# Strassen's seven products for the second MLP product of an attention and MLP kernel, with smaller input rings and a new order

## The chip, the core and the metric

The kernel runs on one core of one Trainium2 chip. The core has a matrix engine (PE), a vector engine (DVE), a scalar engine (ACT), a general engine (POOL) and a queue engine (SP) that here issues transfers. Each engine works through its own instructions in order and waits for the others by semaphores. PE reads SBUF and writes PSUM, which has eight banks; the other engines empty PSUM. The metric is the time of one execution on the device in microseconds (us), as the median of several runs.

## The reference

What is computed, cut to what matters:

```python
# q, k, v: [8, 12, 448, 64]; w_in: [768, 2048]; w_out: [2048, 768]
q_n, k_n = rmsnorm(q, g_q), rmsnorm(k, g_k)
attn = softmax(q_n @ k_n.T / 8)
x = (attn @ v).transpose(0, 2, 1, 3).reshape(3584, 768)
h = x @ w_in
g = h * np.clip(h + 3.0, 0.0, 6.0) / 6.0
return (g @ w_out).astype(np.float32)          # [3584, 768]
```

Eight sequences of 448 tokens with twelve heads of 64 go through attention, and the 3,584 tokens through an MLP of 768 to 2,048 to 768. The "second product" is `g @ w_out`.

## The kernel before

The kernel describes itself as a list of small operations, each with the engines that could run it, what it reads and what it writes (`Plan.add`). Two long tables of numbers then decide everything: `ORDER` is the sequence in which the operations are emitted, and so the order of each engine's queue, and `WAY` picks the second or third of the possible engines where the first isn't used. Waits follow from what is read and written.

Work goes by pairs of heads: six pairs a sequence, 48 in all. For a pair, `load` (L425) brings q, k and v into rings of slots on SP's queue. `prep` squares q and k (L366 on POOL, L364 on ACT), sums the squares on DVE (L454), takes the inverse root on ACT (L430, L433) and scales to bf16 (`qks`, L369, on POOL or DVE). `trans` brings q and k into the layout `T` that PE needs: by PE and copies at first, by transfers from pair 13 on (L561). `score` multiplies (L594; two matmuls of 64 rows side by side), ACT takes the exponential (`eT`, L600), `av` multiplies with v (`X`, L680: 65 columns, the last one the softmax's sum), and `finish` divides on DVE (L696, L699) and transposes into `xT` (L706). The first sequence is treated in halves by functions ending in `_first`, with PE warmed by matmuls on zeros (L382). One line often serves many operations, since helpers such as `copy` (L350 on ACT, L352 on DVE) record them.

The MLP of sequence b runs while the attention of b+1 goes on. `h_group` (L772; L753 for the first sequence) makes 128 of the 2,048 hidden columns with six matmuls of 448 columns into a PSUM bank `M`; ACT applies `relu` (L731, into `ts`), DVE gates (L734) into `gT`, the activations in bf16, with the hidden dimension on partitions. `gT` is a ring of two buffers, each with two sequences: 896 tokens, seven tiles of 128. `y_group` (L794) makes one token tile's row of 768 outputs as two halves of 384 columns, each with 16 matmuls into one bank, in four pieces that `ORDER` can place apart. Each half is copied to a row buffer `y` (three of them), and the row is stored by several transfers (L815). Two banks serve hidden and output products alike, five in the last sequence. `mix` spreads a group's tiles evenly among the next sequence's hidden groups. The last tile's second half is done in two quarters of 192 columns.

Some buffers of the start live inside buffers used later: the first sequence's `T` and v, and two extra q/k slots, in the second `gT`, two extra v slots in `xT`.

Of the kernel before, what the change touches and what calls it, by code (L numbers as in the profile page):

```python
# [12 lines left out]
A_MIN = mybir.AluOpType.min  # L13
LN = mybir.ActivationFunctionType.Ln
# [191 lines left out]
def kernel(  # L206
# [11 lines left out]
    nc = tc.nc  # L218
# [53 lines left out]

    flat = gT_r[1][:].rearrange("p f s -> p (f s)")
    T0 = flat[:, 0:NPAIR * TW].rearrange("p (u c) -> p u c", c=TW)
    o0 = NPAIR * TW
    va0 = flat[0:TP, o0:o0 + NPAIR * 2 * T * E1].rearrange("p (u a t e) -> p u a t e", a=2, t=T, e=E1)
# [683 lines left out]
```

## Time and profile before

| | us |
|---|---|
| median of 3 runs (423.02 to 424.02) | 423.32 |
| profiled execution, first to last instruction | 421.4 |
| PE busy | 413.0 |
| ACT busy | 288.3 |
| PE weight loads busy | 243.8 |
| DVE busy | 233.1 |
| POOL busy | 168.8 |

The profile is one execution of its own. An engine's busy time is the union of its instructions' times; those of PE are pipelined, with modelled ends, so that its busy share alone doesn't tell how full it is. The chain of waits is followed back from the last instruction, at each step to what released it. A group's row names line, engine, operation, output and inputs, shape and count, then busy time, mean length of one in ns, and the idle time before them with what ended it.

### The profile page before, as it was taken

The page shows a single profiled execution, that of the slowest core. Times are in us where ns is not written, and L with a number is a line of the kernel's source. Part 1 is how long each engine was busy: PE and PEld are TensorE (multiplying, and loading weights), DVE is VectorE, ACT ScalarE, POOL GpSimd, SP SyncE. Part 2 cuts the span into 40 slices and gives each one's busy share as a digit, 9 for nine tenths or more (in the row PEclk, how much of TensorE's full clock was granted, in tenths as well). Part 3 has the DMA queues.
Part 4 walks back from the last instruction along what each step waited for, and adds up shares of the span by engine and source line. Part 5 has one row for each costly group of instructions (what it writes and reads, how often), then busy time and mean ns, then how long its engine had stood idle before and what let it go on. Part 6 is the DMA issues. An engine that isn't in the chain of part 4 may idle for free.

```text
span 421.4 us, 9981 instructions
## 1 busy us (share of the span) xinstructions
PE 413.0 (98%) x3959; PEld 243.8 (58%) x3960; DVE 233.1 (55%) x474; ACT 288.3 (68%) x527; POOL 168.8 (40%) x189
## 2 busy tenths in 40 slices
PE   7899999999999999999999999999999999999996
PEld 3566886555545555555555555555655556555565
DVE  5987776588875667536554754447345333333210
ACT  6999887678887988788767876677765662133201
POOL 3999596478374554427344143043210100000000
PEclk9999999999999999999999999999999999999999
DMA  7999999999779799568495683747350601120034
GB/s 241 319 282 196 258 216 177 275 268 271 178 194 252 193 252 242 111 154 211 115 224 160 164 206 73 135 154 166 82 93 12 143 2 47 30 81 27 8 107 114
DMA packets 98979, 67.77 MB, mean 161 GB/s; under 512 B 53204, under 2 KB 95476, under 8 KB 98932
## 3 DMA queue, kind: packets, MB, share of 16 engines
q1 hardware_dynamic: 93296, 60.50, 56.9%
q0 software_dynamic: 5248, 6.29, 9.0%
q8 instruction: 31, 0.51, 0.5%
q10 hardware_dynamic: 388, 0.34, 0.3%
q14 instruction: 16, 0.13, 0.1%
HBM read 50.23 MB, written 11.01 MB: 145 GB/s over the span
## 4 chain that ended last, share of the span: by engine, by line
PE 82%; DMA 7%; ACT 5%; DVE 2%; issue 1%; POOL 1%; SPq 1%; POOLq 0%; ACTq 0%; DVEq 0%
PE M L772 27%; PE M L794 25%; PE X L680 9%; PE S L594 5%; PE M L753 4%; DMA qk<-in_k_dram 4%; PE S L794 4%; PE X L594 3%; DMA T<-qks 2%; PE X L772 1%; ACT sq L364 1%; DMA out_dram<-y 1%; ACT eT L600 1%; ACT eT L622 1%; PE S L617 1%
## 5 line engine op out<-in xcount | busy, mean ns | idle before, releaser
L794 PE MATMUL M<-w_out_sb,gT 128*128 128x384 bf16 x752 | 139.3, 326 | 0.2 <-DMA w_out_sb<-in_moe_w_out_dram 0.2
L772 PE MATMUL M<-xT,w_in_sb 128*128 128x448 bf16 x618 | 135.0, 353 | 0.1
L369 POOL TENSOR_TENSOR qks<-qk,rs 112x512 bf16<-112x512 f32 (+1 forms) x91 | 91.0, 1019 | 107.3 <-ACT rs L433 77.2
L794 PEld LDWEIGHTS <-gT 128*128 128x128 bf16 x912 | 84.5, 98 | 59.5 <-issue 7.6
L734 DVE SCALAR_TENSOR_TENSOR gT<-ts,M 128x448 bf16<-128x448 f32 x119 | 73.2, 616 | 72.1 <-ACT ts L731 71.6
L600 ACT ACTIVATE eT<-S 112x896 bf16<-112x896 f32 x112 | 100.3, 915 | 15.7 <-PE S L594 8.5
L731 ACT ACTIVATE ts<-M 128x448 f32<-128x448 f32 x119 | 64.7, 545 | 42.7 <-PE M L772 29.2
L772 PEld LDWEIGHTS <-w_in_sb 128*128 128x128 bf16 x672 | 60.2, 98 | 56.3 <-issue 10.5
L366 POOL TENSOR_TENSOR sq<-qk 112x512 f32<-112x512 f32 (+1 forms) x57 | 58.0, 1024 | 52.9 <-DMA qk<-in_q_dram 29.7
L680 PEld LDWEIGHTS <-eT 112*128 112x128 bf16 x1344 | 52.7, 97 | 14.5 <-issue 2.0
L600 ACT ACTIVATE eT<-X 112x896 bf16<-112x896 f32 x56 | 51.3, 917 | 13.3 <-PE X L594 12.2
L680 PE MATMUL X<-va,eT 112*128 112x65 bf16 x1344 | 56.0, 194 | 0.1
L454 DVE TENSOR_REDUCE ssq<-sq 112x16 f32<-112x1024 f32 x42 | 50.9, 1213 | 6.1 <-POOL sq L366 4.7
L594 PE MATMUL S<-T 64*128 64x448 bf16 x224 | 34.0, 353 | 0.1
L352 DVE COPY y<-M 128x384 f32<-128x384 f32 x26 | 14.5, 556 | 30.9 <-PE M L794 30.8
L699 DVE TENSOR_TENSOR xn<-X,rd 112x512 bf16<-112x512 f32 x42 | 28.9, 689 | 1.3 <-DVE rd L696 0.2
L696 DVE RECIPROCAL rd<-X 112x8 f32<-112x8 f32 x42 | 8.6, 206 | 34.5 <-PE X L680 28.6
L594 PEld LDWEIGHTS <-T 64*128 64x128 bf16 x336 | 12.9, 94 | 24.5 <-issue 17.2
L364 ACT ACTIVATE sq<-qk 112x512 f32<-112x512 f32 (+1 forms) x40 | 23.0, 586 | 2.8 <-DMA qk<-in_k_dram 2.5
L350 ACT COPY y<-M 128x384 f32<-128x384 f32 x21 | 10.0, 477 | 19.4 <-PE M L794 19.2
L753 PE MATMUL M<-xT,w_in_sb 128*128 128x224 bf16 x192 | 22.9, 259 | 0.0
L794 PE MATMUL S<-w_out_sb,gT 128*128 128x384 bf16 (+1 forms) x128 | 22.6, 316 | 0.0
(87 smaller groups left out, 300.9 us busy)
## 6 DMA issues: line engine op xcount, KB each, us to landing
qk<-in_k_dram SPq DMA_DIRECT2D x45, 256.0 KB, 4.8
qk<-in_q_dram SPq DMA_DIRECT2D x45, 256.0 KB, 4.7
vf<-in_v_dram SPq DMA_DIRECT2D x43, 256.0 KB, 4.8
w_in_sb<-in_moe_w_in_dram POOLq DMA_DIRECT2D x4, 768.0 KB, 8.4
w_out_sb<-in_moe_w_out_dram POOLq DMA_DIRECT2D x4, 768.0 KB, 9.5
out_dram<-y SPq DMA_DIRECT2D x7, 336.0 KB, 3.5
out_dram<-y SPq DMA_DIRECT2D x8, 288.0 KB, 3.3
out_dram<-y SPq DMA_DIRECT2D x8, 240.0 KB, 2.8
```

What stands on the lines that cost most here:

```text
L366: em(nc.gpsimd.tensor_tensor(out=out, in0=in_, in1=in_, op=A_MULT))
L369: em((nc.vector if e == DVE else nc.gpsimd).tensor_tensor(out=out, in0=in_, in1=by.unsqueeze(3).to_broadcast(list(in_.shape)), op=A_MULT))
L454: em(nc.vector.tensor_reduce(out=ssq[:].rearrange("p i n -> p (i n)"), in_=sq[:].rearrange("p i (n d) -> p (i n) d", d=D), axis=AX_X, op=A ...
L594: em(nc.tensor.matmul(out=ps[:, a, 0:S], lhsT=qkT[r, S + t * TP:S + t * TP + 128], rhs=qkT[r, 0:S], start=True, stop=True))
L600: em(nc.scalar.activation(out=eT[:, t, 0:S2].rearrange("p (a s) -> p a s", a=2), in_=ps[0:TP, :, 0:S], func=EXP, bias=0.0, scale=1.0))
L680: em(nc.tensor.matmul(out=X_ps[:, a, i * E1:(i + 1) * E1], lhsT=eT[:, t, c:c + 128], rhs=va[:, a, t, :], start=(t == 0 and i == 0), stop=( ...
L699: em(nc.vector.tensor_tensor(out=xn[:].rearrange("p i a d -> p a i d"), in0=view()[:, :, :, 0:D], in1=rd[:].unsqueeze(3).to_broadcast([TP, ...
L731: em(nc.scalar.activation(out=ts[:], in_=ps()[:, 0:S], func=RELU, bias=0.5, scale=1.0 / 6.0))
L734: em(nc.vector.scalar_tensor_tensor(out=out, in0=shape(ts[:]), scalar=1.0, in1=shape(ps()[:, 0:S]), op0=A_MIN, op1=A_MULT))
L753: em(nc.tensor.matmul(out=ps()[:, f * SH:(f + 1) * SH], lhsT=w_in_sb[:, kt, f0:f0 + 128], rhs=xT[:, kt, z * SH:(z + 1) * SH], start=(kt == ...
L772: em(nc.tensor.matmul(out=ps()[:, 0:S], lhsT=w_in_sb[:, kt, f * 128:(f + 1) * 128], rhs=xT[:, kt, :], start=(kt == 0), stop=(kt == NKT - 1)))
L794: em(nc.tensor.matmul(out=ps()[:, 0:nc0], lhsT=gT[:, f, i * 128:(i + 1) * 128], rhs=w_out_sb[:, f, c0:c0 + nc0], start=(f == 0), stop=(f = ...
```

## The change

For a pair of token tiles, the second product is a 2 x 2 block product: the rows are the tiles i1 and i2, the inner blocks the two halves of the hidden dimension, the columns the two halves of the output. Strassen's scheme makes it with seven products of 8 matmuls of 384 columns each, instead of eight, and needs sums of the operands. A group's seven tiles make three pairs and a single one; the single uses the same changed weights with four products.

- `wsums`: ten sums and differences of blocks of `w_out`, once, of 4 x 384 elements a partition: three new buffers `wb`, and two blocks of `w_out` overwritten in place (`B12`, `B21`).
- `gsum`: five sums of activations for a pair and one for a single, 8 x 128 elements a partition, in bf16, on DVE or POOL; two go to a ring of two buffers `ga`, three in place into `gT`.
- Four products of a pair accumulate two by two in one bank that is read in between; of the outputs some are copied out of PSUM, some added to a row buffer by DVE, and two are differences of row buffers, on POOL or DVE.
- `gT` becomes one buffer with three sequences, in which odd sequences always take the middle third; the start's guests move to the last two thirds. To make room, the q/k ring goes from 5 + 1 slots and 2 extra to 4 + 1 and 1, the v ring from 5 + 1 and 2 to 3 + 1 and 2, and later loads are planned one pair nearer to their use for v.
- `zero_t` is half as wide and read twice. Squares name their two halves as a dimension of their own.
- `mix` takes pairs in portions of 4, 1, 1 and 1 products. `ORDER` and `WAY` are new throughout, for attention and loads also.

The core of the diff (the two tables, the moved guests and renamings left out):

```diff
-    NQK, NV, NSQ, NRS, NQS, NVA, NT, NE, NXN, NXT, NTS, NY = 5, 5, 2, 4, 3, 4, 4, 2, 2, 2, 2, 3
-    NQX = 2
+    NQK, NV, NSQ, NRS, NQS, NVA, NT, NE, NXN, NXT, NTS, NY = 4, 3, 2, 4, 3, 4, 4, 2, 2, 2, 2, 3
+    NG, NC, HF = 3, 2, NFT // 2
+    NQX, NVX = 1, 2
...
-    def y_group(g, i, nb):
...
-        for n, (c0, nc0) in enumerate(cols):
-            ps, res = bank(nb)
-            for part in range(4):
-                def f_y(_, part=part, ps=ps, c0=c0, nc0=nc0):
-                    for f in range(part * 4, part * 4 + 4):
-                        em(nc.tensor.matmul(
-                            out=ps()[:, 0:nc0], lhsT=gT[:, f, i * 128:(i + 1) * 128],
-                            rhs=w_out_sb[:, f, c0:c0 + nc0],
-                            start=(f == 0), stop=(f == NFT - 1)))
...
+    def wsums():
+        fs = HF // 2
+        for j in range(2):
...
+            for n, (o, x, y, op, reads, writes) in enumerate((
+                    (wb[:, 1, lo], b11, b12, A_ADD, [rl], [("wb", 1, j)]),
+                    (wb[:, 2, lo], b21, b22, A_ADD, [rh], [("wb", 2, j)]),
+                    (b12, b12, b22, A_SUB, [rl, rh, ("wb", 1, j)], [("w12", j)]),
+                    (b21, b21, b11, A_SUB, [rl, rh, ("wb", 2, j)], [("w21", j)]),
+                    (wb[:, 0, lo], b11, b22, A_ADD, [rl, rh], [("wb", 0, j)]))):
+                def f_w(e, o=o, x=x, y=y, op=op):
+                    em((nc.vector if e == DVE else nc.gpsimd).tensor_tensor(out=o, in0=x, in1=y, op=op))
+                plan.add("wb", [DVE, POOL], f_w, reads, writes)
...
+    def gsum(g, o, x, y, op, res):
+        def rows(i, k):
+            return gT[:, k * HF:(k + 1) * HF, g_tile(g, i):g_tile(g, i) + 128]
+        out = ga_r[o][:] if isinstance(o, int) else rows(*o)
...
+        def f_s(e):
+            em((nc.vector if e == DVE else nc.gpsimd).tensor_tensor(out=out, in0=rows(*x), in1=rows(*y), op=op))
+        plan.add("ga", [DVE, POOL], f_s, [r for t in (x, y) for f in raw(g, *t)[1] for r in f], wr)
...
+    def product(bk, ab, start=True, stop=True, c0=0, nc0=HALF):
+        ps, res = bk
+        (lhs, rl), (rhs, rr) = ab
+        for j in range(2):
+            def f_y(_, j=j):
+                for f in range(j * 4, j * 4 + 4):
+                    em(nc.tensor.matmul(
+                        out=ps()[:, 0:nc0], lhsT=lhs[f], rhs=rhs[f][:, c0:c0 + nc0],
+                        start=(start and f == 0), stop=(f == HF - 1), skip_group_check=True))
+            plan.add(f"y{nc0}", [PE], f_y, [r for f in range(j * 4, j * 4 + 4) for r in rl[f]] + rr(j), [res])
...
+    def y_add(dst, bk):
+        def f_a(_):
+            em(nc.vector.tensor_tensor(out=dst[0], in0=bk[0]()[:, 0:HALF], in1=dst[0], op=A_ADD))
+        plan.add("yt", [DVE], f_a, [bk[1], dst[1]], [dst[1]])
+    def y_sub(dst, x, y):
+        def f_a(e):
+            em((nc.vector if e == DVE else nc.gpsimd).tensor_tensor(out=dst[0], in0=x[0], in1=y[0], op=A_SUB))
+        plan.add("yu", [POOL, DVE], f_a, [x[1], y[1]], [dst[1]])
...
+    def y_pair(g, i1, i2, nb):
+        row1, row2 = y_row(False), y_row(True)
+        c11, c12, c21, c22 = half(row1, 0), half(row1, 1), half(row2, 0), half(row2, 1)
+        k = [bank(nb), bank(nb)]
+        a6 = gsum(g, 0, (i2, 0), (i1, 0), A_SUB, None)
+        a7 = gsum(g, 1, (i1, 1), (i2, 1), A_SUB, None)
+        a11, a22 = raw(g, i1, 0), raw(g, i2, 1)
+        product(k[0], (a11, B12))
+        y_copy(c22, k[0])
+        product(k[1], (a22, B21))
+        y_add(c22, k[1])
+        a5 = gsum(g, (i1, 1), (i1, 0), (i1, 1), A_ADD, None)
+        a2 = gsum(g, (i2, 0), (i2, 0), (i2, 1), A_ADD, None)
+        product(k[0], (a5, B22), start=False)
+        y_copy(c12, k[0])
+        product(k[1], (a2, B11), start=False)
+        y_copy(c21, k[1])
+        aS = gsum(g, (i1, 0), (i1, 0), (i2, 1), A_ADD, None)
+        yield 4
+        k = bank(nb)
+        product(k, (aS, BSUM))
+        y_add(c22, k)
+        y_sub(c11, c22, c12)
+        y_sub(c22, c22, c21)
+        yield 1
+        k = bank(nb)
+        product(k, (a7, B7))
+        y_add(c11, k)
+        y_store(g, i1, row1, (0, DM))
+        yield 1
+        k = bank(nb)
+        product(k, (a6, B6))
+        y_add(c22, k)
+        y_store(g, i2, row2, (0, DM))
+        yield 1
+    def y_single(g, i, nb, final):
+        row = y_row(True)
+        aS = gsum(g, 0, (i, 0), (i, 1), A_ADD, None)
+        a1, a2 = raw(g, i, 0), raw(g, i, 1)
+        for n, cols in enumerate([[(0, HALF)], [(0, HALF // 2), (HALF // 2, HALF // 2)] if final else [(0, HALF)]]):
+            for c0, nc0 in cols:
+                k = bank(nb)
+                product(k, (a1, B12) if n else (a2, B21), c0=c0, nc0=nc0)
+                product(k, (aS, B22 if n else B11), start=False, c0=c0, nc0=nc0)
+                y_copy(half(row, n, c0, nc0), k, nc0)
...
-        if P + 8 < NP:
-            load(P + 8)
+        if P + 8 < NP:
+            load(P + 8, (0, 1))
+        if P + 7 < NP:
+            load(P + 7, (2,))
```

More of the change, by code (lines that the diff above doesn't have):

```diff
@@ L381, in f_w @@
             for _ in range(n):
-                em(nc.tensor.matmul(out=ps, lhsT=zero_t[:, 0:128], rhs=zero_t[:], start=True, stop=True))
+                em(nc.tensor.matmul(out=ps, lhsT=zero_t[:, 0:128], rhs=zero_t[:].unsqueeze(1).to_broadcast([128, 2, 256]), start=True, stop=True))
         plan.add(kind, [PE], f_w, [], [res])
@@ new lines, with y_row, half, y_copy @@
+    yx = [0]
+    def y_row(single):
+        if not single:
+            return y_r[1], 1
+        yx[0] += 1
+        return y_r[2 * (yx[0] % 2)], 2 * (yx[0] % 2)
+    def half(yrow, n, c0=0, nc0=HALF):
+        return yrow[0][:, n * HALF + c0:n * HALF + c0 + nc0], ("y", yrow[1], n)
+    def y_copy(dst, bk, nc0=HALF):
+        def f_c(e):
+            copy(e, dst[0], bk[0]()[:, 0:nc0])
+        plan.add(f"cy{nc0}", [ACT, DVE], f_c, [bk[1]], [dst[1]])
+    def y_add(dst, bk):
+        def f_a(_):
+            em(nc.vector.tensor_tensor(out=dst[0], in0=bk[0]()[:, 0:HALF], in1=dst[0], op=A_ADD))
+        plan.add("yt", [DVE], f_a, [bk[1], dst[1]], [dst[1]])
@@ L883 @@
             trans_first(P, 0, 1)
-            for n in range(P + 6, min(P + 8, NPAIR + 6)):
-                load(n)
+            if P < 4:
+                load(P + 5)
+                load(P + 6)
+            else:
+                load(P + 5, (0, 1))
     for c in range(NFT // 2):
@@ L901 @@
         h_first(c, 1)
-    for it in ys[1]:
-        y_group(*it, 2)
+    for _ in y_work(ys[1], 2):
+        pass
     done = NPAIR * T
```

187 lines of the change are left out of this document (113 added, 74 removed), and 289 rows, old and new, of tables (ORDER, WAY).

## The prediction

> **What bounds the kernel now.** I read the page's busy times first, then the chain of waits, then windows cut at the ends of the sequences' attention, then the groups by shape.
>
> ```profile
> span 421.4 us, 9981 instructions
> PE 413.0 (98%) x3959; PEld 243.8 (58%) x3960; DVE 233.1 (55%) x474; ACT 288.3 (68%) x527; POOL 168.8 (40%) x189
> PE 82%; DMA 7%; ACT 5%; DVE 2%; issue 1%; POOL 1%; SPq 1%; POOLq 0%; ACTq 0%; DVEq 0%
> ```
>
> TensorE (PE) is busy for 98% of the span and holds 82% of the chain that ended last. A busy PE need not be a full one, so the chain's pieces (start, length, what) have to show it:
>
> ```profile
> 38.45 2.54 ACT eT L600 x3
> 68.28 2.27 DVE ssq L454 x2
> 79.85 6.71 DMA qk<-in_k_dram
> 90.76 7.17 DMA T<-qks
> ...
> 396.71 2.60 PE S L794 x16
> 399.31 0.65 PE X L794 x4
> 399.96 1.30 PE S L794 x8
> 401.26 0.65 PE M L794 x4
> ```
>
> Late in the run each piece begins where the last ended (396.71 + 2.60 = 399.31): nothing but matmuls, at 2.60 / 16 = 0.1625 us for 384 columns. Before about 100 us the chain often leaves PE, for exponentials, reductions and DMAs. So there are two stages: a start in which all engines share the bound, and some 300 us in which a matmul less is its whole time less. The windows (length, then busy us of each engine, clock, DMA share) say how much room the others have:
>
> ```profile
> 7.60:79.50 71.90, 69.31 (x969) 50.45 (x971) 55.13 (x133) 63.54 (x128) 59.38 (x69) 1.00 1.04 246
> 79.50:115.70 36.20, 36.04 (x379) 19.64 (x376) 30.52 (x59) 31.26 (x60) 23.50 (x25) 1.00 1.05 250
> 207.20:258.30 51.10, 51.10 (x470) 28.94 (x467) 28.96 (x53) 37.24 (x67) 20.19 (x20) 1.00 0.71 176
> 357.20:421.40 64.20, 61.00 (x380) 35.90 (x376) 16.43 (x29) 13.61 (x27) 0.00 (x0) 0.99 0.22 61
> ```
>
> The columns are PE, weight loads, DVE, ACT, POOL. Up to the end of the second sequence's attention (79.5 us) ACT has 71.90 - 63.54 = 8.4 us left, POOL 12.5, DVE 16.8. In the middle DVE and POOL stand idle for over 40% of the time; at the end POOL does nothing.
>
> **The change, part by part.**
>
> *Matmuls.* The second product has 28 row tiles x 2 halves x 16 = 896 matmuls of 384 columns. Afterwards twelve pairs take 7 products of 8 and four single tiles 32 each: 672 + 128 = 800. 96 x 0.1625 = **-15.6 us**. Their 96 weight loads go too; loads run beside the matmuls (PEld 58%), so these count nothing. Had the loads been the bound, the price would be the larger of the two, which is still the matmul.
>
> *Sums.* Rows for their prices (busy, mean ns of one | idle before):
>
> ```profile
> L369 POOL TENSOR_TENSOR qks<-qk,rs 112x512 bf16<-112x512 f32 x86 | 88.1, 1043 | 101.2 <-ACT rs L433 71.1 <-DMA T<-qks 17.3 <-issue 12.7
> L369 POOL TENSOR_TENSOR qks<-qk,late_rs 112x256 bf16<-112x256 f32 x5 | 3.0, 605 | 0.0
> L699 DVE TENSOR_TENSOR xn<-X,rd 112x512 bf16<-112x512 f32 x42 | 28.9, 689 | 1.3 <-DVE rd L696 0.2
> L655 DVE TENSOR_TENSOR xn<-XF,rd 112x256 bf16<-112x256 f32 x12 | 4.9, 417 | 0.2
> L352 DVE COPY T<-S 128x448 bf16<-128x448 bf16 x7 | 2.7, 386 | 1.2 <-PE S L542 1.0 <-PE XF L664 0.2
> L352 DVE COPY gT<-M 128x224 bf16<-128x224 bf16 x12 | 3.2, 263 | 0.1
> L352 DVE COPY y<-M 128x384 f32<-128x384 f32 x26 | 14.5, 556 | 30.9 <-PE M L794 30.8
> L734 DVE SCALAR_TENSOR_TENSOR gT<-ts,M 128x448 bf16<-128x448 f32 x119 | 73.2, 616 | 72.1 <-ACT ts L731 71.6
> L369 DVE TENSOR_TENSOR qks<-qk,rs 112x512 bf16<-112x512 f32 x1 | 0.7, 691 | 0.0
> ```
>
> A bf16 sum on DVE is not in the trace. The f32 products grow by (689 - 417) / 256 = 1.06 ns an element, the bf16 copies by (386 - 263) / 224 = 0.55. A token sum of 1,024 elements lies between 0.14 + 0.56 = 0.70 and 0.15 + 1.09 = 1.23 us, a weight sum of 1,536 between 0.98 and 1.78. I take 0.70 and 0.98, as all three operands are 16-bit like the copies'; the others stay for the range. POOL grows by (1043 - 605) / 256 = 1.71 ns: 1.92 us for a token sum, 2.8 for a weight sum, 0.82 for 384 elements; with nothing shorter in the trace, zero growth (1.04) is the lower end.
>
> The order view of the changed kernel puts 36 token sums, 9 weight sums and 8 output differences on DVE, and 28, 1 and 16 on POOL. Output copies fall from 57 (30 on DVE) to 45 (14 on DVE), and 48 additions out of PSUM join on DVE, 0.55 us each by the copy's 556 ns and the gate's 616. DVE: 36 x 0.70 + 9 x 0.98 + 48 x 0.55 + 8 x 0.55 - 16 x 0.556 = 56 us; other work that the order hands from DVE to ACT and POOL takes about 14 off: +42 (+68 with the dear sums). POOL: 28 x 1.92 + 2.8 + 16 x 0.82 = 70, and 12 with what it takes over: +82. ACT: +5. Against a span near 408 that is DVE 275, POOL 251, ACT 293: none is the bound over the whole, and in the middle windows the idle 40% hides it. There I price the sums at nothing; without that cover each costs its own length.
>
> *The start.* Up to the 384th of the 1,536 65-column matmuls (79.5 us today) the new order places, by the same prices, 11.8 us more on DVE (nine weight sums, five token sums, nine more scalings, three additions), 7.8 more on POOL (seven more squares above all) and 7.5 more on ACT (transposed tiles copied there). ACT would fill 63.5 + 7.5 = 71.0 of 71.9 us. It costs between nothing, if all lands in idle time, and 7.5 us, if ACT takes all of it in a row. I charge each at its share of the chain in this stage: ACT's 5% of the chain is 21 us, some 19 of them here, 0.24 x 7.5 = 1.8; DVE's 2% is 8.4 us, 0.11 x 11.8 = 1.3; POOL's 1%, little. **+3.0 us**. DVE's dear prices add 9.8 there (66.9 + 9.8 = 76.7 of 71.9), at most 4.8 of it on the path.
>
> *Banks, and what queues behind a sum.* Banks of the second product are handed over 93 times instead of 57, after 8 matmuls (1.3 us) instead of 16. With two banks each emptying has 1.3 us and takes 0.5, so it hides. The new waits stand on DVE and POOL: a sum into the two-deep ring waits for the product that last read it; behind it on DVE stand gates, output additions and softmax scalings, and PE waits for those. *Slots.* The rings for q and k hold 5 tiles instead of 6, those for v 4 instead of 6. Thirty pairs pass from 115.7 to 357.2 us, 8 us each, so four tiles still give 32 us of lead; the load takes this:
>
> ```profile
> qk<-in_k_dram SPq DMA_DIRECT2D x45, 256.0 KB, 4.8
> ```
>
> Nothing, then; a load that came late would cost up to 4.8 us once, with the transposes behind it on SP. *The tail:*
>
> ```profile
> 417.05 1.15 PE L794 MATMUL X<-w_out_sb,gT 128*128 128x192 bf16 x12
> 418.24 0.32 ACT L350 COPY y<-X 128x192 f32<-128x192 f32 x1 [1.76 <-DMA out_dram<-y]
> 418.58 0.37 ACTq L815 DMA_DIRECT2D out_dram<-y  x1
> ```
>
> The last tile is again a single one that ends in a quarter of 192 columns, so PE's end to the span's end stays 3.2 us; its row buffer was last stored two units earlier, which may hold its first copy. For hand-overs and tail together, 0 to 2, I take **+0.5**.
>
> *Sum:* 421.4 - 15.6 + 3.0 + 0.5 = 409.3 in the profiled execution. That one stands 1.9 us under the median of 423.32, so **411 us**.
>
> **The rivals.**
>
> *A: DVE sums and POOL shut each other out.* The sums on DVE read two operands from SBUF; today's DVE instructions but one read at most one tensor there. That one (the 691 ns row) ran at 5.5 us with POOL idle, so the trace cannot tell. If they exclude each other: in the start DVE has 25 such instructions, 5.0 us of scalings + 9 x 0.98 + 5 x 0.70 + 0.55 = 17.9 us, and POOL is left 12.5 - 7.8 = 4.7 us of idle. 13 us do not fit; POOL works ahead of PE, so I take two thirds, about +8.5: 409.3 + 8.5 + 1.9, **some 419 us**, the more with the dear sums. For it: POOL is the fullest in just this stage. Against it: later POOL is half idle and an exclusion costs at most the rest of one instruction; and six such DVE instructions stand together in the order where no POOL arithmetic starts. The Trainium skill, SBUF — State Buffer, section "SBUF: two separate sides", states this as a rule: a DVE instruction with two SBUF inputs and a GpSimd instruction that reads SBUF hold one port pair in turn, each for its whole length. No run here shows it yet; by that rule the time would be this rival's.
>
> *B, slower: sums in front of what frees a bank.* DVE works in order. If a sum takes 1.23 us and first waits half a POOL instruction (0.5), the gate (0.62) behind it comes 1.7 us late, and PE has only the other bank's 1.1 to 1.3 us. Then each of the 36 DVE sums costs PE about 0.5 us, 18 us together: 411 + 18, **about 429**. It decides from (15.6 - 3.5) / 36 = 0.34 us a sum. For it: DVE's gates already follow ACT closely, with 72 us of idle before them. Against it: the sums need only gates long done, and matmuls of attention stand between the products.
>
> *C: the start gets shorter,* because the instructions before 100 us are ordered differently: without the +3.0 and with 3 us of today's non-PE pieces gone, **405**. Nothing in the profile asks for it.
>
> *D: no change:* the extra start and late sums eat just the 15.6. That needs 12 us more, A and half of B at once.
>
> **How the numbers follow.** Forecast 0.52, its own range 405 to 415; A 0.20 (415 to 422); B 0.20; C 0.05; D 0.03. 0.2% of 423.3 is 0.85 us, about what a measurement of this kernel can tell from no change, so "same" is 422.5 to 424.2: D and the edges of A and B, 0.04. Faster: forecast, C and nearly all of A, 0.76. Slower: B, 0.20. The range takes forecast, C, A and D: 404 to 423; B alone is left out.
>
> **What would show it.** Right: 800 matmuls of 384 columns (two of 192 counting as one) at 0.1625 us; chain pieces abutting from about 105 us on; the end of the second sequence's attention at 80 to 85 us; token sums of 0.70 us on DVE. For A: POOL instructions over 1.04 us, or DVE sums that start as POOL ends, and that mark beyond 88 us. For B: waits of PE for DVE's gates or additions in the middle, over 5 us in sum. Wrong altogether: a time above 422.5.

## The result: 2.7% slower, and the profile after

| | us |
|---|---|
| after, median of 4 runs (432.51 to 436.9) | 434.88 |
| before, beside it, median of 4 runs (423.02 to 424.02) | 423.6 |
| ratio after to before, 95% interval | 1.0268 (1.0229 to 1.0306) |
| profiled execution of after (the fastest of the four): its time, its span | 432.51, 430.7 |

One execution each of e1_slots_head (438.62) and e3_order (436.44) below ran over 1.5% longer than the fastest of its kernel; the ratios leave these two out, and e3_order's trace is of that one.

The page of after, span and busy times:

```profile
span 430.7 us, 9973 instructions
PE 407.3 (95%) x3864; PEld 237.5 (55%) x3864; DVE 293.5 (68%) x520; ACT 292.0 (68%) x539; POOL 270.0 (63%) x250
```

PE has its 96 matmuls less (3,959 records before, 3,864 now, one missing), and yet the span is 9.3 us longer. The chain of waits goes back only to 413.7 us this time and can't show where; windows can. They answer to those of the prediction, cut at the same events: the end of the second and third sequences' attention, and a middle sequence (length, then busy us of PE, weight loads, DVE, ACT, POOL, then clock and DMA).

```profile
7.60:101.04 93.44, 79.03 (x984) 54.85 (x985) 78.98 (x141) 71.40 (x143) 71.03 (x71) 0.93 0.84 201
101.04:134.57 33.53, 32.65 (x353) 17.83 (x351) 25.43 (x47) 28.82 (x55) 27.48 (x31) 1.00 0.98 241
224.08:275.42 51.34, 51.34 (x465) 28.65 (x464) 33.48 (x60) 38.02 (x70) 43.63 (x37) 1.00 0.77 176
```

The first row has it all. The 384th 65-column matmul, at 79.7 us before (the prediction cut at 79.5), ends at 101.0: **21.3 us late**. From there to PE's end it was 418.2 - 79.7 = 338.5 us and is 427.6 - 101.0 = 326.5, **12.0 us less**. In the 21.5 us by which this window is longer, PE is idle 14.4 - 2.6 = 11.8 us more, and busy 79.0 - 69.3 = 9.7 us more for 15 more matmuls (eight of them products of 384 columns, 1.3 us): the clock column fell from 1.00 to 0.93. DVE is busy 79.0 us instead of 55.1.

What the new work costs, in the groups by shape (busy, mean ns of one | idle before):

```profile
L853 DVE TENSOR_TENSOR gT<-gT 128x1024 bf16<-128x1024 bf16 x19 | 21.7, 1146 | 0.0
L853 DVE TENSOR_TENSOR ga<-gT 128x1024 bf16<-128x1024 bf16 x17 | 14.0, 821 | 2.8 <-PE S L873 2.6
L822 DVE TENSOR_TENSOR wb<-w_out_sb 128x1536 bf16<-128x1536 bf16 x6 | 12.1, 2012 | 1.3 <-DMA w_out_sb<-in_moe_w_out_dram 1.3
L822 DVE TENSOR_TENSOR w_out_sb<-w_out_sb 128x1536 bf16<-128x1536 bf16 x3 | 4.4, 1474 | 0.0
L385 POOL TENSOR_TENSOR sq<-qk 112x512 f32<-112x512 f32 x65 | 72.3, 1121 | 29.2 <-DMA qk<-in_q_dram 11.7 <-DVE ssq L473 10.2 <-DMA qk<-in_k_dram 5.9
L853 POOL TENSOR_TENSOR gT<-gT 128x1024 bf16<-128x1024 bf16 x17 | 36.5, 2150 | 14.5 <-DVE ga L853 9.9 <-PE M L873 3.4 <-DMA qk<-in_q_dram 0.7
L822 POOL TENSOR_TENSOR w_out_sb<-w_out_sb 128x1536 bf16<-128x1536 bf16 x1 | 3.1, 3073 | 0.0
```

The mean of a token sum on DVE is 0.82 to 1.15 us and that of a weight sum 1.47 to 2.01, though the shortest of each take 0.64 and 0.95: the same instruction, up to twice as long in the mean. DVE's instructions with one operand in PSUM show nothing of the kind: the 42 products `xn` take 0.68 to 0.69 us each, the 48 additions `y` 0.55 to 0.56. What lies between is seen at 77 us, in the timelines (start, length) of DVE, POOL and PE:

```profile
76.89 1.21 DVE L473 TENSOR_REDUCE ssq<-sq 112x16 f32<-112x1024 f32 x1
78.01 5.08 DVE L822 TENSOR_TENSOR wb<-w_out_sb 128x1536 bf16<-128x1536 bf16 x1
83.02 1.14 DVE L753 SCALAR_TENSOR_TENSOR gT<-ts,M 128x448 bf16<-128x448 f32 x2
84.81 0.95 DVE L822 TENSOR_TENSOR w_out_sb<-w_out_sb 128x1536 bf16<-128x1536 bf16 x1
85.67 0.68 DVE L853 TENSOR_TENSOR gT<-gT 128x1024 bf16<-128x1024 bf16 x1
```

```profile
77.13 2.11 POOL L853 TENSOR_TENSOR ga<-gT 128x1024 bf16<-128x1024 bf16 x1
79.21 3.07 POOL L822 TENSOR_TENSOR w_out_sb<-w_out_sb 128x1536 bf16<-128x1536 bf16 x1
82.23 1.33 POOL L373 CAST va<-vf 112x512 bf16<-112x512 f32 x1
```

```profile
83.68 1.44 PE L873 MATMUL M<-w_out_sb,gT 128*128 128x384 bf16 x4 [2.90 <-DVE gT L753]
```

DVE takes up the weight sum at 78.01, while POOL is at a token sum; as that ends, POOL goes on at once to its own weight sum, and DVE's ends at 83.09, 0.81 us after that one: nearly its whole own length lies behind POOL's. Five microseconds for 0.95. The gates behind it on DVE come at 83.02, and PE waited 2.90 us for them. Between 84 and 86 us, with POOL idle, the same sums take 0.95 and 0.68.

How much of this there is, I add up as *lengthening*: each DVE and POOL instruction's length less the shortest of its shape. From 40 to 101 us it is 10.8 us on DVE and 5.5 on POOL; before, in the same stretch, 1.4 and 0.6.

The clock, in windows of after and (last two rows) of before:

```profile
20.00:26.00 6.00, 3.42 (x52) 2.41 (x50) 6.00 (x12) 4.67 (x9) 5.98 (x7) 0.92 0.92 181
26.00:30.00 4.00, 3.81 (x45) 2.43 (x44) 3.31 (x13) 1.94 (x3) 2.18 (x4) 0.50 1.05 276
78.00:84.00 6.00, 2.10 (x18) 1.05 (x17) 6.00 (x4) 4.81 (x9) 5.57 (x3) 0.93 0.80 263
84.00:86.00 2.00, 2.00 (x19) 1.48 (x18) 1.97 (x4) 0.00 (x0) 0.00 (x0) 0.50 0.00 0
```

```profile
20.00:26.00 6.00, 5.97 (x127) 4.37 (x124) 5.44 (x22) 5.94 (x10) 6.00 (x9) 1.00 1.01 211
26.00:30.00 4.00, 4.00 (x75) 2.75 (x71) 3.29 (x8) 3.97 (x9) 3.82 (x6) 1.00 1.01 335
```

A stretch in which PE stands still for half the time is followed by one at half clock: in 26 to 30 us PE does 45 matmuls where before it did 75. An idle PE is paid for twice. Up to the 384th 65-column matmul the clock stands at half from 11.4 to 14.8, 25.1 to 31.9 and 83.1 to 86.5 us, 13.7 us in all, and before the change never; by an estimate from these stretches that is at most 13.7 / 2 = 6.8 of the 9.7 us.

For the rest of the run, the view of PE's waits from 101 us on (in total, times, longest) has no more than this:

```profile
PE M L797 <- DMA xT<-xn: 0.8, 1, 0.8
PE M L797 <- DVE gT L753: 0.7, 1, 0.7
PE S L873 <- DVE y L897: 0.6, 1, 0.6
PE M L873 <- DVE y L897: 0.6, 1, 0.6
PE M L873 <- DVE gT L753: 0.5, 2, 0.3
```

The marks on the way divide the start. The 96th 65-column matmul ends at 37.3 us (before 25.6), the 192nd at 48.2 (36.4), the 384th at 101.0 (79.7): 11.7 us are lost by the 96th, nothing more up to the 192nd, and 9.6 us behind it. The first of all sums on DVE or POOL starts only here:

```profile
62.32 0.95 DVE L822 TENSOR_TENSOR wb<-w_out_sb 128x1536 bf16<-128x1536 bf16 x1
```

No sum can have caused the first 11.7 us. Some of DVE's scalings in them also read two operands from SBUF and are lengthened, by 2.7 us together (1.55 us instead of 0.68 for the worst, at 23.59). So the question is the start: is it the mutual exclusion of DVE's sums and POOL, the fewer input slots, the new order of the attention's operations, or the work as such?

### The profile page after: what moved, and what is told of

Same layout as the page of the kernel before. It is cut to its first block, busy times and chain, and to the rows that moved or that the text cites. A ratio compares the mean times of both kernels' runs of the same rounds, so it can differ in the third digit from the quotient of the medians.

```text
span 430.7 us, 9973 instructions
## 1 busy us (share of the span) xinstructions
PE 407.3 (95%) x3864; PEld 237.5 (55%) x3864; DVE 293.5 (68%) x520; ACT 292.0 (68%) x539; POOL 270.0 (63%) x250
## 5 line engine op out<-in xcount | busy, mean ns | idle before, releaser
L388 POOL TENSOR_TENSOR qks<-qk,rs 112x512 bf16<-112x512 f32 (+1 forms) x88 | 92.9, 1070 | 41.6 <-ACT rs L452 38.4
L753 DVE SCALAR_TENSOR_TENSOR gT<-ts,M 128x448 bf16<-128x448 f32 x120 | 73.7, 616 | 56.9 <-ACT ts L750 55.7
L385 POOL TENSOR_TENSOR sq<-qk 112x512 f32<-112x512 f32 (+1 forms) x69 | 74.8, 1092 | 30.6 <-DMA qk<-in_q_dram 13.1
L873 PE MATMUL M<-w_out_sb,gT 128*128 128x384 bf16 (+1 forms) x384 | 70.6, 325 | 4.0 <-DVE gT L753 3.2
L873 PEld LDWEIGHTS <-gT 128*128 128x128 bf16 x552 | 51.0, 98 | 42.3 <-issue 11.1
L853 POOL TENSOR_TENSOR gT<-gT 128x1024 bf16<-128x1024 bf16 x17 | 36.5, 2150 | 14.5 <-DVE ga L853 9.9
L897 DVE TENSOR_TENSOR y<-M,y 128x384 f32<-128x384 f32 x40 | 22.2, 554 | 17.9 <-PE M L873 12.3
L873 PEld LDWEIGHTS <-ga 128*128 128x128 bf16 x264 | 24.6, 98 | 17.6 <-issue 2.8
L369 ACT COPY y<-M 128x384 f32<-128x384 f32 (+1 forms) x26 | 12.1, 467 | 26.1 <-PE M L873 21.1
L853 POOL TENSOR_TENSOR ga<-gT 128x1024 bf16<-128x1024 bf16 x11 | 23.8, 2164 | 6.5 <-PE M L873 4.0
L873 PE MATMUL M<-wb,ga 128*128 128x384 bf16 x144 | 27.2, 326 | 0.2 <-DVE gT L753 0.2
## 6 DMA issues: line engine op xcount, KB each, us to landing
w_out_sb<-in_moe_w_out_dram POOLq DMA_DIRECT2D x4, 768.0 KB, 10.8
```

What stands on the lines that cost most here:

```text
L385: em(nc.gpsimd.tensor_tensor(out=out, in0=in_, in1=in_, op=A_MULT))
L388: em((nc.vector if e == DVE else nc.gpsimd).tensor_tensor(out=out, in0=in_, in1=by.unsqueeze(3).to_broadcast(list(in_.shape)), op=A_MULT))
L753: em(nc.vector.scalar_tensor_tensor(out=out, in0=shape(ts[:]), scalar=1.0, in1=shape(ps()[:, 0:S]), op0=A_MIN, op1=A_MULT))
L853: em((nc.vector if e == DVE else nc.gpsimd).tensor_tensor(out=out, in0=rows(*x), in1=rows(*y), op=op))
L873: em(nc.tensor.matmul(out=ps()[:, 0:nc0], lhsT=lhs[f], rhs=rhs[f][:, c0:c0 + nc0], start=(start and f == 0), stop=(f == HF - 1), skip_grou ...
```

## The experiments

Times stand against the kernel before on the same chip; "mark" is the end of the 384th 65-column matmul (before 79.7, after 101.0).

**One part of the start at a time.** Four kernels, run together. The first takes the room of `wb`, unused until the weight sums, for input tiles:

```diff
-    NQX, NVX = 1, 2
+    NQX, NVX = 3, 4
...
+    wbf = wb[:].rearrange("p n f c -> p (n f c)").bitcast(FP32)
...
-    wsums()
...
+    wsums()
```

(two q/k tiles and two v tiles in `wbf`; the calls of `wsums` follow the first pairs' preparation; the first weight sum waits for those tiles' readers.)

> Four more input tiles at the start (two for q and k, two for v), laid in the room of the weight sums before these are written, so that eight pairs can be loaded ahead as in the kernel before, and not six; the order is that of the changed kernel. Theory S (the fewer slots hold the loads back: SP waits 58.1 us for POOL's scalings before 105 us, against 22.1 before the change): those waits fall below 30 us, the 384th 65-column matmul ends by 95 us instead of 101.0, and the time falls from 434.9 to about 428. Theory X (DVE's two-input sums and POOL shut each other out): the time stays within 2 us of 434.9, with the 5.09 us weight sum still there. Theory O (the order and the engines of the first 37 us): within 2 us of 434.9, with the 96th mark still at about 37 us.

Measured: 434.01 us (433.47 to 434.58), ratio 1.0243 (1.0226 to 1.0260); mark 101.8. Up to 105 us SP waits 56.9 us for POOL's scalings as against 58.1, and the 5.08-us weight sum is there again, at 78.8. More slots alone give nothing: POOL frees a slot no sooner.

The second makes DVE's sums one-input instructions of the same length. The sums that DVE forms are left out thereby: a part of one operand is copied. Memsets of `wb` and `ga` at the start cost some 1.2 us.

```diff
+                    if e == DVE:
+                        em(nc.vector.tensor_scalar(o[:, :, 0:192], x[:, :, 0:192], 1.0, None, A_MULT, A_ADD, accum_out=junk_t[:]))
...
+            if e == DVE:
+                em(nc.vector.tensor_scalar(out[:, :, 0:64], rows(*x)[:, :, 0:64], 1.0, None, A_MULT, A_ADD, accum_out=junk_t[:]))
```

> All token and weight sums that DVE has in the changed kernel become instructions of the same length with one SBUF input (a copy with an accumulated output over half the columns: 512 for a token sum, 768 for a weight sum), so that part of the sums is left out. Order, engines and slots stay. Theory X: these copies take their 0.7 and 0.95 us whatever POOL does, no DVE instruction of the sums is over 1.1 us, the 384th mark falls from 101.0 to about 92 us and the time from 434.9 to about 425. Theories S and O: the marks move by under 2 us, and the time stays above 432.

Measured: 429.5 us (424.67 to 430.24), ratio 1.0106 (1.0040 to 1.0173); mark 97.3. Its groups by shape:

```profile
L862 DVE TENSOR_SCALAR_CACHE_REDUCE gT<-gT 128x512 bf16<-128x512 bf16 x19 | 12.9, 676 | 0.1
L862 DVE TENSOR_SCALAR_CACHE_REDUCE ga<-gT 128x512 bf16<-128x512 bf16 x17 | 11.5, 679 | 2.9 <-PE S L884 2.6
L390 POOL TENSOR_TENSOR sq<-qk 112x512 f32<-112x512 f32 x65 | 67.7, 1050 | 26.8 <-DVE ssq L478 12.1 <-DMA qk<-in_q_dram 10.5 <-DMA qk<-in_k_dram 4.0
```

Instructions of the same length at the same places, but with one input: DVE's now take 0.68 us each and POOL's squares 1,050 ns instead of 1,121. The lengthening from 40 to 101 us falls to 1.6 on DVE and 0.7 on POOL. That is the exclusion of the sums, shown by itself, and in this order it is worth 434.9 - 429.5 = 5.4 us (the ratio's interval is 2.8 us to each side), not twenty, and little over half of what theory X expected. The new instructions also move fewer elements; but a sum of 0.95 us that lasts until POOL stops, above and below, does not look like shared traffic. From the 192nd matmul to the mark it is 48.0 us now, 52.9 in after and 43.3 before: the exclusion is about half, 4.9, of the 9.6 us lost there.

The third gives the operations up to the 96th 65-column matmul the order and engines that they had before (`ORDER` and `WAY` alone); the fourth is that with the four input tiles.

> The changed kernel with the order and the engines of the kernel before up to the 96th 65-column matmul (243 operations, all of them in both kernels; three loads that have no free slot yet are issued as soon as they have one), then its own order. Theory O: the 96th mark falls from 37.3 to about 26 us, and nearly all of that stays to the end: about 425. Theory S: the 96th mark falls as well, but the 384th by less than half as much, as the loads of the second sequence still wait for slots: about 430. Theory X: the first 37 us hold only 5 us of lengthened instructions, so the 96th mark stays above 32 us and the time above 430.

> Both of the other edits: four more input tiles at the start, and the order and engines of the kernel before up to the 96th 65-column matmul. If order and slots are both at work and add: 96th mark about 26 us, 384th about 86, time about 418. If the order alone: the same as with the old head alone, about 425. If exclusion rules: above 430.

Measured: e1_head 433.74 us (432.88 to 434.48), ratio 1.0236 (1.0214 to 1.0257); e1_slots_head 428.14 (427.43 to 438.62), 1.0099 (1.0080 to 1.0118). In e1_head the 96th 65-column matmul ends at 25.2 us, as before the change (25.6) and 12 us earlier than after: the new order and choice of engines up to there, and not the slots, cost the first 11.7 us. By the mark (101.2) all of it is lost again. The timelines of DVE, POOL and PE in e1_head show to what:

```profile
66.78 0.61 DVE L754 SCALAR_TENSOR_TENSOR gT<-ts,M 128x448 bf16<-128x448 f32 x1
67.31 8.64 DVE L823 TENSOR_TENSOR wb<-w_out_sb 128x1536 bf16<-128x1536 bf16 x1
```

```profile
65.48 3.03 POOL L386 TENSOR_TENSOR sq<-qk 112x512 f32<-112x512 f32 x3
68.47 1.03 POOL L389 TENSOR_TENSOR qks<-qk,rs 112x512 bf16<-112x512 f32 x1
69.47 1.03 POOL L386 TENSOR_TENSOR sq<-qk 112x512 f32<-112x512 f32 x1
70.47 1.03 POOL L389 TENSOR_TENSOR qks<-qk,rs 112x512 bf16<-112x512 f32 x1
71.46 0.60 POOL L374 CAST va<-vf 112x512 bf16<-112x512 f32 x1
72.03 1.03 POOL L389 TENSOR_TENSOR qks<-qk,rs 112x512 bf16<-112x512 f32 x1
73.03 2.11 POOL L854 TENSOR_TENSOR ga<-gT 128x1024 bf16<-128x1024 bf16 x1
76.03 3.10 POOL L823 TENSOR_TENSOR w_out_sb<-w_out_sb 128x1536 bf16<-128x1536 bf16 x1 [0.90 <-DVE wb L823]
```

```profile
PE M L779 <- DVE gT L754: 6.4, 1, 6.4
```

A weight sum of 0.95 us stands 8.64 us on DVE, while POOL runs seven more instructions without a gap; it ends 0.8 us after POOL first stops, for want of just this sum. PE lost 6.4 us to the gate behind it. Slots and head together bring 6.7 us, alone 0.9 and 1.1: each removed wait uncovers the next, and their gains do not add up.

**More of before's order, and all parts at once.** e2_slots_head192 is e1_slots_head with before's order up to the 192nd 65-column matmul. e2_all is that with the one-input sums of e1_one_input (so DVE's sums are left out in it too).

> Four more input tiles at the start as in the run with slots, and the order and engines of the kernel before up to the 192nd 65-column matmul instead of the 96th. If the head's order and the slots hold the start back: 192nd mark 36 to 38 us (43.3 with the cut at the 96th), 384th about 88, time about 421. If what follows bounds it anyway (sums and POOL shutting each other out from 55 to 100 us): 384th mark above 93 us and a time above 426.

> The run with slots and the old order up to the 192nd matmul, and DVE's token and weight sums as one-input instructions of the same length (half of the sums is left out, and the products with weight sums read half their columns twice). If order, slots and exclusion together are the cause and add: 384th mark 80 to 84 us and a time of 411 to 415, near the forecast. If something else lengthens the start, for instance the plain number of instructions on DVE between 55 and 100 us: 384th mark above 88 us and a time above 419.

Measured: 429.19 us (427.49 to 431.24), ratio 1.0124 (1.0074 to 1.0175), mark 95.7; and 423.48 (421.66 to 426.54), 0.9990 (0.9959 to 1.0021), mark 97.7. With all three suspects removed the kernel is as fast as before, no faster. The one-input sums are worth 429.2 - 423.5 = 5.7 us in this order, much as in the other. The trace of e2_all is of the slowest of its ten executions (426.54), and there PE's largest wait is this:

```profile
PE M L787 <- DMA w_in_sb<-in_moe_w_in_dram: 7.8, 3, 4.0
```

The last two loads of `w_in` are issued about when they were before (34.6 and 36.1 us; 34.5 and 38.0) but land at 48.5 and 54.3 instead of 42.3 and 46.9, beside loads of `w_out` that start at 40.9 instead of 54.1. I take this for a fault of the joined orders; it is not shown.

**Smaller causes.** e2_wsum_dve puts POOL's single weight sum, the one at 79.21 above, on DVE (one entry of `WAY`):

```diff
-    11: 1, 63: 1, 73: 2, 75: 1, 79: 1, 90: 1, 93: 1, 98: 1, 99: 1, 100: 2, 104: 1, 109: 1, 110: 1, 111: 2,
+    63: 1, 73: 2, 75: 1, 79: 1, 90: 1, 93: 1, 98: 1, 99: 1, 100: 2, 104: 1, 109: 1, 110: 1, 111: 2,
```

e2_plain multiplies the first two sequences' tiles as before, by eight products of eight (24 matmuls more), and forms the weight sums only then; `ORDER` and `WAY` are those of before up to the 800th 65-column matmul; the four input tiles are in it.

```diff
+    PLAIN = [(0, 0, 1), (0, 2), (0, 3, 4), (0, 5, 6)]
...
+            if u in PLAIN:
+                yield from y_plain(u[0], u[1:], nb)
+                continue
+            if not summed:
+                summed.append(1)
+                wsums()
```

> The changed kernel with the one weight sum that POOL does (3.07 us) given to DVE; nothing else. Theory X: the 5.09 us weight sum on DVE stood behind that instruction and the token sum before it; it falls under 3 us, PE's wait of 2.9 us at 83 us shrinks, and 2 to 4 us come off: 431 to 433. Theories O and S: within 1.5 us of 434.9.

> A version of its own: the seven row tiles of the first two sequences are multiplied plainly as before the change (three pairs fewer by seven products: 24 more matmuls of 384 columns, 3.9 us), so that the weight sums are not needed before some 160 us; they are spread over 86 to 165 us, all on DVE. Four more input tiles at the start, the order of the kernel before up to the 800th 65-column matmul, then that of the changed kernel. If the loss sits in the start and comes of sums, slots and order there: 384th mark 79 to 82 us, time about 413 to 416 (423.3 - 15.6 + 3.9 + 1 to 4). If the gain of the seven products is lost elsewhere: 384th mark as low, but a time above 419.

Measured: e2_wsum_dve 432.17 us (431.63 to 433.12), 1.0184 (1.0155 to 1.0213): 2.7 us for one instruction moved, though the slowest of the four (433.12) is above the fastest of after (432.51); the 5.08-us sum is 2.04 us there. e2_plain 450.92 (449.02 to 451.94), 1.0618 (1.0582 to 1.0655). Its start is the point: the mark is at **84.1** us. With neither the sums nor the new order in the start, the start is nearly what it was; this run doesn't tell the two apart. Behind it its order, joined from two, has PE wait 19.0 us for gates; as a kernel it is of no use.

**Orders searched anew.** A search over `ORDER` and `WAY` moved operations against a simple model of the engines, with durations from these traces. e3_order keeps DVE's two-input instructions and POOL's apart in that model; e3_blind is the same search without this; e3_before applies it to the kernel before; e3_slots_order is e3_order with the four input tiles.

> The changed kernel, same operations and same tiles, with another order and another choice of engine where there is one. The order comes from a new search that uses the durations of the traces (token sum 0.69 us on DVE and 2.12 on POOL, weight sum 0.95 and 3.07, squares and scalings 1.04 on POOL, product of four matmuls 0.65) and that never lets a two-input sum on DVE and a POOL instruction run at once. Theory X+O (the loss is an order that did not know of the exclusion): 384th mark 78 to 86 us instead of 101.0, DVE's sums hardly lengthened (under 5 us over the run, 22 in the changed kernel), time 405 to 414. Rival W (the sums and the squares are too much work for DVE and POOL before the 384th mark in any order): mark above 92 us and time above 425.

> The same search with the same durations and the same length, except that sums on DVE and POOL's instructions are taken to run side by side. Theory X (the exclusion is what costs): DVE's sums are lengthened again by over 10 us in all, and the time is 8 to 20 us above that of the order that knows of it. Rival O (a poor order, whatever the reason; the exclusion is a side effect): within 4 us of that order.

> Control: the kernel before with an order from the same search. If the search alone is better than the one that made the two kernels, it gains here too: 410 to 418. If the order of the kernel before was already good, as its start suggests: 419 to 425. The difference between this and the first run of the batch is then what the change itself is worth under equal care.

> Four more input tiles at the start, and an order from the same search for that kernel. Theory S (six pairs loaded ahead are too few): at least 3 us less than the first run of the batch. Otherwise (six are enough once the order fits): within 2 us of it.

| | us (range) | ratio to before | mark |
|---|---|---|---|
| e3_order | 431.28 (429.73 to 436.44) | 1.0171 (1.0148 to 1.0194) | 96.0 |
| e3_blind | 461.86 (461.2 to 464.39) | 1.0914 (1.0887 to 1.0941) | 112.3 |
| e3_before | 445.18 (444.53 to 445.86) | 1.0506 (1.0488 to 1.0524) | 88.0 |
| e3_slots_order | 433.89 (433.35 to 435.29) | 1.0243 (1.0223 to 1.0263) | 93.1 |

The weight sums on DVE, by shape, of e3_order and of e3_blind:

```profile
L825 DVE TENSOR_TENSOR wb<-w_out_sb 128x1536 bf16<-128x1536 bf16 x5 | 5.6, 1128 | 2.5 <-DMA w_out_sb<-in_moe_w_out_dram 2.5
L825 DVE TENSOR_TENSOR w_out_sb<-w_out_sb 128x1536 bf16<-128x1536 bf16 x4 | 3.8, 949 | 0.0
```

```profile
L824 DVE TENSOR_TENSOR wb<-w_out_sb 128x1536 bf16<-128x1536 bf16 x4 | 13.4, 3342 | 0.6 <-DMA w_out_sb<-in_moe_w_out_dram 0.6
L824 DVE TENSOR_TENSOR w_out_sb<-w_out_sb 128x1536 bf16<-128x1536 bf16 x3 | 11.3, 3780 | 0.0
```

e3_order missed its 405 to 414, and its mark of 78 to 86; e3_slots_order is 2.6 us slower, so more slots do not help here. Two searches that differ in one assumption differ by 30.6 us, and the sums by 1.1 and 0.95 against 3.3 and 3.8 us each. And the control: the same search makes the kernel before 21 us slower, the changed one 3.6 faster. Between the two searched kernels lie 445.2 - 431.3 = 13.9 us in favour of the change: its mark is 8.0 us later, and from there to PE's end it takes 335.0 us instead of 351.2. The search's order is worse than the one that the kernel before has, and it is one search of each, so this is a hint that the products' saving stands behind the mark, not a price of the change.

A second search also counted half clock, eight loads under way and the switching cost told below. e4_order and e4_slots (with the input tiles) result from it, e4_blind is e4_slots with the exclusion ignored, e4_before the kernel before.

> The changed kernel, same operations, tiles and slots, with an order from a second search. It counts what the first batch of searched orders showed on the chip and the first search had left out: PE at half clock for 3.4 us and more after a stretch of 3.4 us in which it worked under some 60%; 0.19 us for each run of 64-row score matmuls set between others (158 such runs in the first searched order, 94 in the changed kernel, 88 in the one before); loads that land 0.74 us apart, at most eight under way. Sums on DVE never beside POOL. Theory X+O+C (exclusion, and the idle PE and half clock that follow, in an order made without them): 384th mark 79 to 84 us, granted clock at 1.0 from 15 us on, time 405 to 413, the forecast's. Rival W (too much work before the mark in any order): mark above 90, time above 420.

> The same search with four more input tiles at the start. Theory S (six pairs loaded ahead are too few): at least 3 us below the run with six. Otherwise: within 2 us of it.

> As the run with four more tiles, from the same first order with a search of the same length, but with the sums on DVE and POOL's instructions taken to run side by side; clock, score runs and loads counted as there. Theory X: at least 15 us above that run, DVE's sums lengthened by over 15 us in all, 384th mark above 92 us. Rival O (any order made with the clock and the loads in mind does): within 5 us of it.

> Control: the kernel before, with an order from the same second search. 419 to 424 if its order was as good as this search can make it; if it falls below 415, the search and not the change explains what the other runs gain.

Measured: 435.75 us (434.19 to 437.39), 445.4 (444.41 to 449.31), 447.55 (445.04 to 448.39) and 443.59 (441.45 to 445.65); ratios 1.0284 (1.0263 to 1.0305), 1.0524 (1.0493 to 1.0554), 1.0551 (1.0528 to 1.0574) and 1.0461 (1.0435 to 1.0487); marks 103.6, 110.9, 107.6 and 98.4. All four missed, and they have one thing in common: the search had moved the weight loads to the front, the first to 4 or 5 us instead of 16 before the change and 20 after it. The DMA queues of e4_before from 10 to 36 us (packets, MB, share):

```profile
q0 software_dynamic: 2857, 3.11, 69.2%
q1 hardware_dynamic: 3577, 3.45, 46.6%
```

q0 carries the weights from POOL's queue, q1 the inputs. In this stretch the input loads of 256 KB landed about 2.2 us apart, and 0.75 us apart where no weight load is under way. PE starved (5.4 of 10 us busy from 15 to 25 us) and its clock fell (0.74 there). Exclusion or not then made 2 us. Beside e4_before, e4_order is 7.8 us faster and e4_slots 1.8 us slower, with the same change: single searches scatter too much to price it.

**The start alone, with the weight loads left in place.** e5_head searches only the operations up to about 110 us, from e2_slots_head192 on, and also punishes sums that wait for an idle POOL; e5_whole searches the whole.

> The changed kernel with the four more input tiles (as in e1_slots), and with the order and the engine choices of the operations up to about 110 us searched once more; behind them the changed kernel's own order stands. The search started from the order of e2_slots_head192, let DVE's two-input sums and POOL's instructions run only one after the other, counted eight loads at a time, half clock after partly idle stretches and the cost of switching into score matmuls, left the weight loads where they are, and also had to come out well when a DVE sum waits until POOL is idle. Theory O (the start was lost by an order that sets the sums against POOL's and DVE's other work): the 384th 65-column matmul ends at 80 to 88 us (before 79.7, after 101.0, e1_slots_head 94.8), a few score matmuls show half clock, and the rest takes the changed kernel's 326.5 us: PE ends at 407 to 415 and the time is 411 to 420 us, below the kernel before. Theory W (the added work itself does not fit into the start, whatever the order): the mark stays at 92 us or more, and the time at 425 to 434 us.

> As e5_head, but the search may move the operations of the whole run, weight loads left out. Theory O: the 384th mark at 81 to 89 us, and from there to PE's end no more than the changed kernel's 326.5 us: 411 to 420 us. Theory W: mark at 92 us or more, 425 us or more. If the mark is early and the rest takes over 330 us, the search's own middle is at fault, as in e3_order and e3_before, and e5_head tells the start by itself.

Measured: e5_head 433.3 us (432.51 to 436.04), ratio 1.0241 (1.0209 to 1.0274), mark 102.1; e5_whole 432.31 (431.48 to 433.93), 1.0204 (1.0176 to 1.0232), mark 99.0. Theory O falls in this form, and by its numbers theory W holds. But not for W's reason: from 40 to 101 us DVE's lengthening is 5.6 us instead of 10.8, and the time went elsewhere. Timelines of DVE and POOL and the largest wait of PE in e5_head:

```profile
61.57 1.90 DVE L830 TENSOR_TENSOR wb<-w_out_sb 128x1536 bf16<-128x1536 bf16 x1 [5.24 <-DMA w_out_sb<-in_moe_w_out_dram]
63.40 0.61 DVE L761 SCALAR_TENSOR_TENSOR gT<-ts,M 128x448 bf16<-128x448 f32 x1
```

```profile
56.20 3.10 POOL L830 TENSOR_TENSOR wb<-w_out_sb 128x1536 bf16<-128x1536 bf16 x1 [4.66 <-DMA w_out_sb<-in_moe_w_out_dram]
```

```profile
PE M L786 <- DVE gT L761: 5.0, 1, 5.0
```

The new order set weight sums where `w_out` had not landed yet. DVE stood 5.24 us, POOL 4.66, PE 5.0 behind DVE's next gate, and half clock followed. As I read it, a weight sum has to come after its load, before its product, beside an idle POOL and not in front of an urgent gate, and this start offers few such places. e3_order had them (1.1 and 0.95 us a sum) and still had its mark at 96.0, with other waits in their stead.

## Why the prediction was wrong

**The matmuls, -15.6: right.** The records count 784 products of 384 columns and 32 of 192, which make 800. Ahead of the mark there are eight more than before the change, 1.3 us of the 21.3; behind it 104 less, 16.9 us, of which 12.0 appear. Of the 4.9 that don't, PE's idle time there takes 2.9 (3.4 us instead of 0.5), and more switching, told below, about 1.

**The sums in the middle at nothing: right.** From 224 to 275 us PE is busy 51.34 of 51.34 us. The durations taken were those of the instructions alone (0.70 for 0.68, 0.98 for 0.95, 1.92 for 2.11 and 2.8 for 3.07 on POOL); the dear bounds weren't needed. The sign of rival B, more than 5 us of PE's waits for gates and additions, came to 0.7 + 0.6 + 0.6 + 0.5 = 2.4: B fell, in the middle. Its picture of a sum in front of a gate is right, but in the start.

**The start, +3.0: this is the step that failed.** Measured: +21.3. It put 11.8 us more on DVE, 66.9 us in a start of 72 to 75, and charged each engine's additional length at that engine's share of the chain. DVE was busy 79.0 us in 93.4. Two things failed in it. It priced the new order by busy time alone and had no term for an order in which PE waits and then runs at half clock: 11.7 us were lost by the 96th matmul, ahead of every sum, and e1_head, with before's order and engines up to there, doesn't lose them. And it took the sums' lengths as fixed and the engines as independent, while the sums made two engines into one for as long as they ran: e1_one_input shows this for 4.9 of the 9.6 us between the 192nd matmul and the mark. The other 4.7 stay open. e2_plain, with before's order and no sums in its start, has its mark at 84.1, 4.4 us behind before.

**Rival A had the mechanism and too small a price.** Its signs all came: POOL's squares at 1,121 ns, sums that end just after POOL does, the mark beyond 88, though more than half of that delay stands ahead of the first sum. The Trainium skill, SBUF — State Buffer, section "SBUF: two separate sides", has the rule, that a two-input DVE instruction and a GpSimd instruction which reads SBUF hold a shared port pair in turn; the trace agrees, with 0.68 us becoming 1.15 on average. I weighed against it that an exclusion costs at most the rest of one instruction. That was the mistake inside A: the waits were 5.08 and 8.64 us long, two and eight POOL instructions, since POOL ran on. And I priced the overflow of busy time, 8.5 us, but neither the gate queued behind a sum nor the clock that falls when PE then idles. With the exclusion of the sums removed 5.4 us go in one order and 5.7 in another; between a search that knew of it and one that didn't lay 30.6 us in e3 and 2 in e4: its price is a matter of order.

**Slots at nothing: right alone, wrong together.** Four more tiles made 0.9 us in after's order and 433.7 - 428.1 = 5.6 once the head was quick; in both searches the kernel with them was the slower one.

**Hand-overs and tail, +0.5: right within its 0 to 2.** PE waits 1.2 us for output additions behind the mark, and from PE's end to the span's end there are 430.7 - 427.6 = 3.1 us.

**What stays open.** Exclusion, slots and head together account for 434.9 - 423.5 = 11.4 us. The forecast lies another 12.5 below that. e2_all's wait for `w_in`, 7.8 us in its slowest execution, is part of that; how long its other executions wait is not known, and a kernel near 416 is not shown. How much half clock costs by itself was not tried. No version of the changed kernel that computes the whole beat the kernel before; the nearest was e1_slots_head, 428.14 us.

## What to carry to other kernels

Before adding two-input DVE work, look at what POOL does in the same microseconds: where POOL runs without gaps, price such an instruction not at its length but at the time until POOL next stops, and then look at who stands behind it. A saving on the engine that is the bound late in the run is safe there, but the preparations it needs fall into the start, where the other engines are fullest and a pause of PE also costs clock. A new order of the start needs a price of its own: here it cost 11.7 us before the first sum ran. When one removed cause gives nothing, remove two together before acquitting either, and run the same treatment on the kernel before as a control.

## What the runs showed of the hardware that was not expected

- **No turn for a waiting DVE instruction.** At 67.31 us of e1_head it waited through seven further POOL instructions and began only when POOL had nothing to run; elsewhere (68.21 us of after) it got in after one, and took 1.79 us. What decides between them, the traces don't say.
- **Half clock without a long pause.** In after, PE was busy 3.42 of 6 us from 20 us on, and 2.10 of 6 from 78 on, and then ran at 0.50. The Trainium skill, TensorE: Matmul & The Clock Gate, section "HAM oscillation — how this bites in real kernels", warns of pauses over some 3.4 us; the longest single wait of PE here is 2.9 us, so a stretch that is half idle was enough. The clock records of these traces change in steps of 3.41 us; wherever a step at full clock was followed by one at half, PE had been busy for at most 57% of it, and no step with PE busy for less than 45% was followed by full clock.
- **Switching into and out of 64-row matmuls.** A 448-column matmul follows another after 0.189 us; from 128 rows to 64 rows, and back, the step is 0.28 us, about 0.095 more each way. After has 94 runs of score matmuls instead of 88, e3_order 158: 64 x 0.19 = 12 us more.
- **Weight loads slow input loads.** In e4_before 256 KB landed 0.75 us apart alone (at 36.68 and 37.43 us), about 2.2 us apart beside a 768 KB load from POOL's queue (at 17.64, 19.80 and 21.98).
